# Top-k attention with a PReLU MLP: the MLP step ahead of the scores in a single block's tick, and k's copy at the end of PE's tick

## The chip, the cores and the metric

The kernel runs on 1 core of one Trainium2 chip. The metric is the device time of one execution in microseconds (us). Beside the times there is a profile: one execution recorded by the hardware profiler, with every instruction of the engines PE (TensorE), ACT (ScalarE), DVE (VectorE), POOL (GpSimd) and SP (SyncE, which here only issues DMAs).

## What is computed

The reference, cut to what matters. q, k and v are (8, 8, 576, 64) in float32: 8 batches of 8 heads of 576 rows.

```python
scores = scale * np.matmul(q, k.transpose(0, 1, 3, 2))
kth = np.partition(scores, -32, axis=-1)[..., -32:-31]
scores = np.where(scores >= kth, scores, -1e9)          # the 32 largest of each row of 576
attn = exp(scores - max(scores)); attn /= attn.sum() + 1e-9
x = matmul(attn, v)  ->  (8*576, 8*64)                  # 4608 tokens of 512
h = x @ w_in                                            # 512 -> 2048
out = (max(h, 0) + alpha * min(h, 0)) @ w_out           # 2048 -> 512
```

## The kernel before

**Tiling.** Two heads make a *pair*; there are 32 pairs, four to a batch. The 576 query rows of a pair's two heads are cut into nine *row blocks* of 128 rows: eight blocks of one head each (j = 0 to 7, heads alternating) and a ninth (j = 8) that holds the last 64 rows of both heads. A row block's scores are 128 x 576. There are 288 row blocks, and the schedule is a loop of ticks (line 861): in tick n each engine does its part for the row blocks that have come to it.

**Units.** Row blocks 0-1, 2-3, 4-5 and 6-7 go in units of two, and block 8 alone. The text calls block 8 a *single*, and its tick the single's tick. `scores(n0)` (line 312) does the score matmuls of a whole unit into PSUM tiles `ps` (two buffers). A unit of two needs both buffers, so the second of its tiles can only be written when ACT has copied the tile before it out.

**What each engine does with a row block.** PE: scores. ACT: `act_b` (L340, copies the scores to b with a per-row bias), `act_s` (L346, counts by sign how many are above a limit, the tile named h), `act_e` (L351, exp, once for a unit). POOL turns the count into a flip flag SG (L356). DVE then flips (y, L362), takes the 8 largest of five segments (L373), merges them (L387, L389), finds the limit, and makes the mask (mk, L436). POOL multiplies mask and exp (w, L446), and a DMA transposes w into wT (L459). PE multiplies wT by v (`av`, L497), DVE takes reciprocals of the sums (rz) and ACT scales the result into xb (L526). After the fourth pair of a batch, xb is transposed into xT by DMA and the MLP of that batch's tokens is queued.

**The MLP queue.** `back` is a list of MLP steps, at most one of which PE starts in a tick of the main part (lines 893 to 904). There are two kinds: a *ph step* (`ph_step`, L721: w_in times x into PSUM, after which ACT's relu, L727, makes gT) and a *pz step* (`pz_step`, L735 and L739: a third of the sum over w_id and w_out; after the third, ACT's L744 copies it to o_sb and SP writes it out). Each step goes into the one PSUM buffer "misc", so a new ph step, or the first third of a pz, waits until ACT has emptied it. ACT's part of a step (relu or copy) is put into `after` and is the first thing ACT does in the next tick. In the first 150 us the queue holds the preparation of the weights instead (`weight_steps`: L652 on ACT, L661 on PE).

**The preparation of a pair** (`prep_plan`, line 176) is laid out by hand over 14 ticks ahead of the pair's first row block: q's transposes on PE (`pe_q`, L198), their copy on ACT (`act_q`, L201) and k's transposes on PE (`pe_k`, L209) in the next tick, k's copy on ACT (`act_k`, L213) and the two remaining transposes (`pe_t`, L217 and L218) in the one after, then `act_t` (L221) and `pe_g` (L226), then `act_g` (L230, GK) and `pe_r` (L239, pr). All of them use one PSUM buffer "pa" in turn, up to pr, which has two banks of its own kind. `dve_p` (L245, L247: P from pr) follows on DVE a tick later. For nearly all pairs `pe_k` falls in a tick with j = 5, `act_k` in the next, j = 6, `act_g` and `pe_r` in the single's tick, and `dve_p` in the tick after it, j = 0. Pairs 11 and 20 (LEAD1, LEAD2) are four ticks earlier and use "misc".

**The order within a tick**, which is the order of each engine's instructions: PE does `scores(n + 1)`, if a unit starts at n + 1, then the MLP step, then `run(n, "pe")`: what the plan has put there (av, pe_q, pe_k, pe_r and so on). ACT does `after`, then `act_b` of a unit that starts at n; in a tick that starts a unit of two the plan's ACT work comes next and then `act_s`, in the unit's second tick `act_s`, the plan's ACT work and `act_e`, in a single's tick `act_b`, `act_s`, the plan's ACT work and `act_e`.

The ticks from 252 on (N0: the last four pairs) have another order of row blocks.

Of the kernel before, what the change touches and what calls it, by code (L numbers as in the profile page):

```python
# [31 lines left out]
def kernel(  # L32
# [20 lines left out]
    NT = NPAIR * TPP  # L53
# [7 lines left out]
    N0 = P0 * TPP  # L61
# [102 lines left out]
    n = 0  # L164
# [11 lines left out]
    def prep_plan(p):  # L176
# [117 lines left out]
        else:  # L294
            ts = [-14, -13, -12, -11, -10, -9, -7, -6, -5, -5, -4, -4, -3, -2, -8]
        dvx = "dve" if p < 2 else "dvx"
        steps = [dict(pe=[pe_q]), dict(act=[act_q], pe=[pe_k]), dict(act=[act_k], pe=[pe_t]),
                 dict(act=[act_t], pe=[pe_g]), dict(act=[act_g], pe=[pe_r]),
                 dict(dve=[dve_p]), dict(pe=[pe_s]), dict(act=[act_m]), dict(dve=[dve_2]),
                 {dvx: [dve_3]}, dict(dve=[dve_4]), {dvx: [dve_4b]}, dict(dve=[dve_5]),  # L300
# [473 lines left out]
    with tc.manual_schedule(engines={E.PE, E.Activation, E.DVE, E.Pool, E.SP}):  # L774
        cal = {}

        def put(tick, eng, f):
            cal.setdefault((tick, eng), []).append(f)

        def run(tick, eng):  # L780
            for f in cal.pop((tick, eng), ()):
                f()

        def plan(p):
            for dt, st in prep_plan(p):
                for eng, fs in st.items():
                    for f in fs:
                        put(BASE[p] + dt, eng, f)

        def feed(lim):  # L790
            while blocks and blocks[0][0] + blocks[0][1] <= lim:
                back.extend(mlp_steps(*blocks.pop(0)))

        def flush():
            while back:
                pe_f, act_f, _, takes = back.popleft()
                if takes and len(after) >= 2:
                    after.popleft()()
                pe_f()
                if act_f:  # L800
                    after.append(act_f)
            while after:
                after.popleft()()

        def tail_of(n, wn):
            wp, wj = ORDER[wn]
            b = wp // KPB
            if wp < P0:
                if wj == 3:
                    put(n + 3, "pe", lambda: av(wp, 0))  # L810
                    put(n + 4, "dve", lambda: av_rz(wp, 0))
                    put(n + 6, "act", lambda: av_out(wp, 0))
                    if wp % KPB == KPB - 1 and b >= 5:
                        put(n + 6, "end", lambda: x_turn(b, (0, 1)))
                        put(n + 8, "end", lambda: feed(b * S + 256))
                if wj == 8:
                    put(n + 4, "pe", lambda: av(wp, 1))
                    put(n + 5, "dve", lambda: av_rz(wp, 1))
                    put(n + 7, "act", lambda: av_out(wp, 1))
                    if wp % KPB == KPB - 1:  # L820
                        put(n + 7, "end", lambda: x_turn(b, range(2 if b >= 5 else 0, 5)))
                        put(n + 9, "end", lambda: feed((b + 1) * S))
            elif (wj == 8 or wj % 2) and wp % 2:
                i, g = wj // 2, (wp - P0) // 2
                dt = 2
                if i == 3 and g == 1:
                    put(n + dt, "pe", flush)
                put(n + dt, "pe", lambda: av_last(i, g))
                where = "end" if i == 3 and g == 0 else "dvx"
                put(n + dt + 1, where if where == "end" else "dve", lambda: rz_last(i, g))  # L830
                put(n + dt + 1, where, lambda: out_last(i, g))
                if i == 3:
                    if g == 1:
                        put(n + dt + 1, where, lambda: last_ph(0))
                    put(n + dt + 2 - g, where, lambda: turn_last(g))
                    if g == 1:
                        put(n + dt + 1, where, lambda: (last_ph(1), last_pz()))
                elif g == 1:
                    put(n + dt + 1, "dvx", lambda: x_turn(b, (i,)))
                    put(n + dt + 2, "end", lambda: back.extend(mlp_steps(*last.pop(i))))  # L840

        load(0, nc.scalar)
        load(1)
        load_alpha()
        plan(0)
        plan(1)
        early_sets()
        load_v(0)
        for t in range(-16, 0):
            for eng in ("act", "pool", "pe", "dve"):  # L850
                run(t, eng)
        scores(0)
        back = deque((a, c, 1.0, 0) for a, c in weight_steps())
        credit = 0.0
        after = deque()
        wdue, held = {}, []
        for wn in range(NT):
            wdue.setdefault(wn + LAG_W if wn < NW else 3 * (wn // 3) + 7, []).append(wn)
        n = 0
        end = max(NT + 24, 0)  # L860
        while n < end or back or after:
            if 8 <= n < 12:
                put(n, "end", lambda i=n - 8: load_v(1, [i]))
            for p in range(2, NPAIR):
                if n == max(0, BASE[p] - 18):
                    load(p)
                    plan(p)
                if n == max(0, BASE[p] - 13):
                    load_v(p)
            banks[0] = 2 if n >= NT else 1 if n >= N0 + 2 else 0  # L870
            if n + 1 < NT and unit_of[n + 1][2] == 0:
                scores(n + 1)
            while after:
                after.popleft()()
            if n < NT:
                n0, m, i = unit_of[n]
                if i == 0:
                    act_b(n0)
                    if m == 2:
                        run(n, "act")  # L880
                    act_s(n)
                    if m == 1:
                        run(n, "act")
                        act_e(n0)
                else:
                    act_s(n)
                    run(n, "act")
                    act_e(n0)
            run(n, "act")
            if n >= 3 and n % 3 == 0 and n - 3 < NT:  # L890
                sel_a((n - 3) // 3)
            nb = 1 if n < N0 + 2 else 2
            credit = min(credit, 0.0) + (2.4 if n >= NT else 1.9)
            first = True
            while back and credit > 0.0 and (first or nb == 2):
                pe_f, act_f, cost, takes = back[0]
                if takes and len(after) >= nb:
                    break
                back.popleft()
                pe_f()  # L900
                if act_f:
                    after.append(act_f)
                credit -= cost
                first = False
            run(n, "pe")
            if n >= NT:
                run(n, "dve")
                run(n, "dvx")
            due = wdue.get(n, ())
            for wn in due:  # L910
                if wn < NW:
                    mask(wn)
            for f in held:
                f()
            held = []
            for wn in due:
                weights(wn, wn >= NW)
                tail_of(n, wn)
            if 0 <= n - 1 < NT:
                side_of(n - 1)  # L920
            segs = seg_ops(n - LAG_S) if 0 <= n - LAG_S < NT else []
            mn = n - LAG_M
            merges = merge_ops(mn) if 0 <= mn < NT else []
            pick = bool(merges) and mn % 3 == 2
            if pick and n >= NT:
                sel_eq(mn // 3)
            lm = n - LAG_M - 3
            for i in range(max(len(segs), len(merges), 2)):
                if i < len(segs):
                    segs[i]()  # L930
                if i < len(merges):
                    merges[i]()
            run(n, "dve")
            if 0 <= lm < NT and lm % 3 == 0:
                limit(lm // 3)
            if pick and n < NT:
                sel_eq(mn // 3)
            if 0 <= n - 1 < NT:
                flip(n - 1)
            run(n, "dvx")  # L940
            if pick:
                sel_pr(mn // 3)
                held = [lambda m=mn // 3: sel_sum(m)]
                if mn % TPP == TPP - 1:
                    put(n + 2, "dve" if mn < NT - 1 else "end", lambda g=mn // TPP: check_group(g))
                    if mn == NT - 1:
                        put(n + 2, "end", checks)
                        put(n + 3, "end", final_flag)
                        put(n + 7, "end", read_flag)
            run(n, "end")  # L950
            n += 1
        assert not cal and not blocks and not last
# [138 lines left out]
```

## Time and profile before

| | us |
|---|---|
| time, median of 3 runs | 866.85 |
| the 3 runs | 864.89, 866.85, 867.13 |
| the profiled execution, its own time | 866.57 |
| its span, first to last instruction | 864.7 |
| PE busy with matmuls in the span | 711.5 (82%) |
| DVE busy | 817.5 (95%) |
| ACT busy | 783.7 (91%) |
| POOL busy | 443.6 (51%) |

The span is 1.87 us shorter than the execution's own time. The mean clock that the throttle granted to TensorE is 0.928 of full speed.

How to read the rows that follow. A row of the timeline gives the start in us from the span's start, the duration in us, the engine, the line of the kernel, the operation, out<-in, the shape, and how many equal instructions are merged in the row; in brackets the idle time of the engine just before it and what ended it. A row of the waits gives engine, line and tile, then what was waited for, then us in total, how often, and the longest. A matmul's end is modelled and overlaps the next one, and ACT's instructions overlap their neighbours by about 0.1 us. Float32 score matmuls appear as two instructions each, so a unit of two is x8.

### The profile page before, as it was taken

Reading aid. Unit: us, or ns where it says so; the run is one execution under the profiler, and the core shown is the slowest. Engines: PE = TensorE matmul, PEld = TensorE weight load, DVE = VectorE, ACT = ScalarE, POOL = GpSimd, SP = SyncE. Lnnn points to the kernel's source line nnn. Section 1 sums busy time; section 2 is a strip of 40 time slices with the busy share of each in tenths; the row PEclk is TensorE's granted clock in tenths of the full one; section 3 lists DMA queues with packets and bytes.
Section 4 is the critical chain, followed back from the end, with each engine's and each line's share of the span. In section 5 each row is a group of like instructions: output and inputs, shape, how many; then the busy total and the mean of one; then the engine's idle time right before and its main releaser. Section 6 shows DMA issues by size and latency. Waiting matters only on the chain. (4 is left out here: it accounts for less than half of the span.)

```text
span 864.7 us, 20335 instructions
## 1 busy us (share of the span) xinstructions
PE 711.5 (82%) x5696; PEld 424.3 (49%) x5771; DVE 817.5 (95%) x4901; ACT 783.7 (91%) x1865; POOL 443.6 (51%) x643
## 2 busy tenths in 40 slices
PE   5767688778968789877988789977897879899996
PEld 3434454434544445544454345644455455566674
DVE  5999999999999999999999999999999999998991
ACT  5989999989999999999999999999999799989861
POOL 5565555545545555554555545555555555554530
PEclk9666879889999999999997999999999899899998
DMA  7799965544775555564576456565456544435452
GB/s 144 141 162 183 168 116 102 120 97 87 137 142 119 91 116 127 108 123 90 116 162 113 96 97 130 110 126 104 100 116 126 114 100 90 94 77 96 100 91 52
DMA packets 343002, 99.06 MB, mean 115 GB/s; under 512 B 335056, under 2 KB 335328, under 8 KB 342880
## 3 DMA queue, kind: packets, MB, share of 16 engines
q1 hardware_dynamic: 338096, 94.99, 55.9%
q0 software_dynamic: 3584, 2.39, 2.2%
q8 instruction: 47, 0.77, 0.4%
q14 instruction: 75, 0.61, 0.2%
q10 hardware_dynamic: 1200, 0.30, 0.2%
HBM read 36.71 MB, written 9.44 MB: 53 GB/s over the span
## 5 line engine op out<-in xcount | busy, mean ns | idle before, releaser
L446 POOL TENSOR_TENSOR w<-mk,e 128x576 bf16<-128x576 bf16 x250 | 318.8, 1275 | 327.4 <-DVE mk L436 185.1
L373 DVE MAX8 C<-y 128x8 f32<-128x112 f32 (+1 forms) x1440 | 381.6, 265 | 0.1
L331 PE MATMUL ps<-qkT 64*128 64x288 f32 (+1 forms) x1280 | 254.1, 470 | 34.5 <-ACT b L340 33.8
L340 ACT ACTIVATE b<-ps,NT 128x576 f32<-128x576 f32 x288 | 202.1, 760 | 7.8 <-PE ps L331 7.8
L346 ACT ACTIVATE h<-b 128x576 bf16<-128x576 f32 x288 | 203.1, 705 | 1.6
L721 PE MATMUL ph<-xT,w_in_b 128*128 128x128 bf16 (+2 forms) x997 | 147.6, 289 | 41.6 <-ACT gT L727 38.4
L331 PEld LDWEIGHTS ps<-qkT 64*128 64x128 f32 (+1 forms) x1280 | 132.4, 192 | 95.4 <-ACT b L340 57.8
L351 ACT ACTIVATE e<-b 128x1152 bf16<-128x1152 f32 (+1 forms) x158 | 174.4, 1104 | 0.0
L362 DVE TENSOR_SCALAR y<-b,SG 128x576 int32<-128x576 int32 x288 | 149.4, 519 | 10.2 <-POOL SG L356 7.9
L387 DVE MAX8 L<-C 128x8 f32<-128x40 f32 x864 | 156.7, 181 | 0.1
L436 DVE TENSOR_SCALAR mk<-b,KP 128x576 bf16<-128x576 f32 x282 | 144.0, 511 | 0.0
L739 PE MATMUL pz<-w_out_b,gT 128*128 128x512 bf16 x542 | 132.6, 380 | 1.2 <-issue 0.5
L721 PEld LDWEIGHTS <-w_in_b 128*128 128x128 bf16 x1024 | 79.8, 99 | 104.2 <-issue 80.3
L727 ACT ACTIVATE gT<-ph 128x512 bf16<-128x512 f32 x140 | 85.8, 620 | 23.6 <-PE ph L721 23.4
L389 DVE MATCH_REPLACE8 C<-L,C 128x40 f32<-128x40 f32 x576 | 104.4, 181 | 0.0
L739 PEld LDWEIGHTS <-gT 128*128 128x128 bf16 x560 | 51.7, 98 | 68.9 <-issue 14.7
L497 PE MATMUL pu<-v_bf,wT 128*128 128x65 bf16 (+1 forms) x1600 | 68.8, 198 | 9.5 <-DMA wT<-w 9.1
L497 PEld LDWEIGHTS <-wT 128*128 128x128 bf16 (+1 forms) x1600 | 64.7, 103 | 18.8 <-DMA wT<-w 9.5
L356 POOL TENSOR_SCALAR SG<-S_all 128x1 int32<-128x1 f32 x288 | 64.8, 225 | 3.8 <-ACT h L346 3.5
L446 POOL TENSOR_TENSOR wm<-mk,e 128x576 bf16<-128x576 bf16 x32 | 40.8, 1276 | 46.3 <-DVE mk L436 43.7
L346 ACT ACTIVATION_READ_ACCUMULATOR h<-b 128x1 f32 x288 | 63.0, 219 | 0.0
L526 ACT ACTIVATE xb<-pu,rz 128x64 bf16<-128x64 f32 x224 | 54.4, 369 | 0.0
(116 smaller groups left out, 734.6 us busy)
## 6 DMA issues: line engine op xcount, KB each, us to landing
out_dram<-o_sb SPq DMA_DIRECT2D x34, 256.0 KB, 2.2
st_q<-in_q_dram SPq DMA_DIRECT2D x64, 128.0 KB, 2.8
kst<-in_k_dram SPq DMA_DIRECT2D x62, 128.0 KB, 2.9
st_v<-in_v_dram SPq DMA_DIRECT2D x60, 128.0 KB, 2.6
w_stage<-in_moe_w_out_dram SPq DMA_DIRECT2D x16, 256.0 KB, 3.2
w_in_b<-in_moe_w_in_dram POOLq DMA_DIRECT2D x8, 256.0 KB, 5.8
wT<-w SPq DMA_TRANSPOSE x128, 3.3
st_q<-in_q_dram SPq DMA_DIRECT2D x32, 32.0 KB, 2.6
```

The lines of the kernel that those rows point to most:

```text
L331: nc.tensor.matmul(o_, l_, r_, start=True, stop=True)
L340: nc.scalar.activation(t["b"].rearrange("p (a c) -> p a c", a=2), t["ps"], AF.Identity, bias=NT0[:, p * TPP + j:p * TPP + j + 1], scale=ON ...
L346: nc.scalar.activation(h, tiles[n]["b"], AF.Sign, accum_out=S_all[:, n:n + 1])
L351: nc.scalar.activation(e, tiles[n0]["bu"], AF.Exp, scale=scl)
L362: nc.vector.tensor_scalar(t["y"].bitcast(I32), t["b"].bitcast(I32), FLIP, SG[:, n:n + 1], ALU.bitwise_xor, ALU.bitwise_xor)
L373: return [lambda g=g: nc.vector.max(out=C[:, n % TPP, g, :], in_=y[:, g:S // 8:NSEG, :]) for g in range(NSEG)]
L387: ops.append(lambda r=r, src=src: nc.vector.max(out=L[:, 8 * r:8 * r + 8], in_=src))
L436: nc.vector.tensor_scalar(t["mk"], t["b"], row_limit(n), None, ALU.is_ge)
L446: nc.gpsimd.tensor_tensor(dst, t["mk"], t["e"], ALU.mult)
L497: nc.tensor.matmul(o_, wT[:, 4 * side + c, cs], d["v"][:, 5 * side + c, :], start=(c == 0), stop=(c == 4))
L721: nc.tensor.matmul(hold[f][:, i, :], w_in_b[:, kk, (f + i) * 128:(f + i + 1) * 128], xT[:, kk, c0:c0 + tb], start=(kk == 0), stop=(kk == N ...
L739: nc.tensor.matmul(pz[0:m], hold["gT"][:, f, r0:r0 + m], w_out_b[:, f, :], start=False, stop=(f == NFT - 1))
```

## The change

Two things move; no instruction is added or taken away.

1. In the tick of a single (j = 8) before tick 252, where the next unit's scores are due, `scores(n + 1)` is now emitted behind the MLP step of that tick instead of ahead of it. The plan's PE work (`pe_r`) still comes last. That is 28 ticks, one for each pair up to the 28th. In all other ticks the scores stay first.
2. `act_k` moves from the plan's ACT work of the tick after `pe_k` to a new slot "actz" at the end of ACT's work in the tick of `pe_k` itself. On ACT's queue it now stands ahead of the next tick's `after` and `act_b`, and behind `act_e`. This holds for pairs 1 to 31; pair 0 has a plan of its own.

```diff
-        steps = [dict(pe=[pe_q]), dict(act=[act_q], pe=[pe_k]), dict(act=[act_k], pe=[pe_t]),
+        steps = [dict(pe=[pe_q]), dict(act=[act_q], pe=[pe_k], actz=[act_k]), dict(pe=[pe_t]),
...
-            if n + 1 < NT and unit_of[n + 1][2] == 0:
+            nxt = n + 1 < NT and unit_of[n + 1][2] == 0
+            late = nxt and n < N0 and unit_of[n][1] == 1
+            if nxt and not late:
                 scores(n + 1)
             while after:
                 after.popleft()()
...
                 credit -= cost
                 first = False
+            if late:
+                scores(n + 1)
             run(n, "pe")
+            run(n, "actz")
```

## The prediction, made before the changed kernel was run

> **What bounds the kernel now.** First the page: which engine is full, and what the chain that ended last is made of.
>
> ```profile
> PE 711.5 (82%) x5696; PEld 424.3 (49%) x5771; DVE 817.5 (95%) x4901; ACT 783.7 (91%) x1865; POOL 443.6 (51%) x643
> ...
> PE 12%; ACT 4%; DVE 1%; issue 0%; DVEq 0%
> ```
>
> DVE is nearly full, yet the chain that ended last holds 16% of the span on PE and ACT and 1% on DVE: the last stretch hangs on when PE and ACT get there. So two things run side by side, DVE, and a loop of PE and ACT that wait for one another. Second, the waits from 130 us (first MLP steps) to 730 us (the last tick that the change touches), ACT's and then DVE's:
>
> ```profile
> ACT gT L727 <- PE ph L721: 18.1, 18, 2.7
> ACT o_sb L744 <- PE pz L739: 9.2, 6, 1.6
> ```
>
> ```profile
> DVE P L247 <- PE pr L239: 9.3, 11, 1.9
> ```
>
> ACT waits only for PE here, never for DVE, so ACT and PE go at a pace of their own; DVE loses 9.3 us in 11 waits for pr, which PE makes in a single's tick, and under 1.5 us in smaller rows. What PE and ACT gain reaches the end, as long as DVE follows; DVE can follow by about those 9.3 to 10.5 us.
>
> Third, the timeline of one single's tick whose MLP step is a ph step; ACT, PE, DVE:
>
> ```profile
> 391.20 0.68 ACT L727 ACTIVATE gT<-ph 128x512 bf16<-128x512 f32 x1
> 391.67 0.83 ACT L340 ACTIVATE b<-ps,NT 128x576 f32<-128x576 f32 x1
> ...
> 393.38 0.67 ACT L351 ACTIVATE e<-b 128x576 bf16<-128x576 f32 x1
> 394.80 0.60 ACT L727 ACTIVATE gT<-ph 128x512 bf16<-128x512 f32 x1 [0.75 <-PE ph L721]
> 395.29 1.36 ACT L340 ACTIVATE b<-ps,NT 128x576 f32<-128x576 f32 x2
> ```
>
> ```profile
> 392.56 1.24 PE L331 MATMUL ps<-qkT 64*128 64x288 f32 x6 [1.73 <-ACT b L340]
> 393.72 1.04 PE L721 MATMUL ph<-xT,w_in_b 128*128 128x512 bf16 x4
> 394.69 0.44 PE L239 MATMUL pr<-qkT,GK 64*64 64x512 bf16 x4
> ```
>
> ```profile
> 395.15 0.82 DVE L247 TENSOR_TENSOR P<-pr,qkT 128x512 bf16<-128x512 f32 x2 [0.86 <-PE pr L239]
> ```
>
> PE idles 1.73 us until the single's b has freed the second score buffer, does the scores, and only then ph, whose buffer had been free since the relu ended at 391.88. ACT runs dry for ph and DVE for pr.
>
> **The change part by part. Part 1, ph singles.** After it, ph starts at the relu's end, about 391.93, and ends near 392.95, beside b; the scores follow (b ended at 392.50) to about 394.2, then pr to 394.6 instead of 395.13. ACT's gT starts at e's end, its 0.75 us of waiting gone; b comes 0.5 us behind gT's start, at about 394.5, and the scores are there by 0.3 us. That margin is the cover; without it the wait moves to b. Of the 18 gT waits, four stand at the head of a single's tick, on the ph of the tick before, and stay; the first and the last of them:
>
> ```profile
> 159.66 0.60 ACT L727 ACTIVATE gT<-ph 128x512 bf16<-128x512 f32 x1 [0.95 <-PE ph L721]
> ...
> 569.95 0.60 ACT L727 ACTIVATE gT<-ph 128x512 bf16<-128x512 f32 x1 [0.59 <-PE ph L721]
> ```
>
> With the two between, 2.7 us. The other 14 hold 15.4. Three of these are long because PE ran at half clock, here the one at 676 us (rows of PE, of ACT, and the stretch with its granted clock, 0.50, as the third number from the end), then ACT's rows of the other two:
>
> ```profile
> 672.05 2.29 PE L331 MATMUL ps<-qkT 64*128 64x288 f32 x6 [1.71 <-ACT b L340]
> 674.27 1.89 PE L721 MATMUL ph<-xT,w_in_b 128*128 128x256 bf16 x8
> ```
>
> ```profile
> 676.20 0.60 ACT L727 ACTIVATE gT<-ph 128x512 bf16<-128x512 f32 x1 [2.65 <-PE ph L721]
> ```
>
> ```profile
> 672.00:677.90 5.90, 5.56 (x20) 2.90 (x22) 5.53 (x34) 3.22 (x7) 2.92 (x4) 0.50 0.59 122
> ```
>
> ```profile
> 191.46 0.60 ACT L727 ACTIVATE gT<-ph 128x512 bf16<-128x512 f32 x1 [2.65 <-PE ph L721]
> ...
> 497.73 0.60 ACT L727 ACTIVATE gT<-ph 128x512 bf16<-128x512 f32 x1 [2.21 <-PE ph L721]
> ```
>
> Eleven at full clock: 15.4 - 2.65 - 2.21 - 2.65 = **7.9 us**, all gained by ACT. In the three slow ones, kept slow, the scores end last: 1.9 for ph from 0.6 ahead of b's end, 2.3 for the scores, so ACT's b can start 3.6 after the single's b, against 4.7: 1.1 us in one, 1.85 in the half-slow one at 497, and 0.5 in the one at 676, where PE itself is behind afterwards. Together **3.4 us**; with the clock at full they would give 7.5, with none of it kept 0.
>
> **Part 1, pz singles.** Six singles (one in each batch from 213 us, the last at 725) have a pz step. ACT, then PE:
>
> ```profile
> 416.67 0.62 ACT L744 COPY o_sb<-pz 128x512 f32<-128x512 f32 x1
> 417.13 0.80 ACT L340 ACTIVATE b<-ps,NT 128x576 f32<-128x576 f32 x1
> ...
> 419.38 1.36 ACT L340 ACTIVATE b<-ps,NT 128x576 f32<-128x576 f32 x2
> ...
> 425.43 0.58 ACT L744 COPY o_sb<-pz 128x512 f32<-128x512 f32 x1 [1.51 <-PE pz L739]
> ```
>
> ```profile
> 417.98 1.24 PE L331 MATMUL ps<-qkT 64*128 64x288 f32 x6 [0.81 <-ACT b L340]
> 419.15 1.04 PE L735 MATMUL pz<-w_id_b,xT 128*128 128x512 bf16 x4
> 420.02 0.81 PE L739 MATMUL pz<-w_out_b,gT 128*128 128x512 bf16 x3
> 420.76 0.44 PE L239 MATMUL pr<-qkT,GK 64*64 64x512 bf16 x4
> ```
>
> Here ACT didn't wait: b started at 419.38 with its scores ready. Now pz runs from 417.35 to 418.96, the scores to 420.2, pr to 420.5. So **b waits 0.85 us that it didn't wait before**, and behind it on ACT stand h and e of that unit. But pr and all that follows on PE come 0.7 us earlier, and 6 us later ACT stands 1.51 us waiting for PE's pz (the o_sb waits, 9.2 us in 6): the lost 0.85 is eaten there, and PE's 0.7 comes through. 6 x 0.7 = **4.2 us**; if the o_sb wait didn't cover it, it would be 6 x 0.85 = 5.1 lost instead. At 726 us PE becomes the chain that ends last, so the sixth counts in full too.
>
> Singles without an MLP step stay as they are. `scores` issues no DMA; the DMAs and POOL work of the weight steps that it is moved behind keep their order on SP and POOL.
>
> **Part 2, k's copy.** It costs 0.5 us on ACT wherever it stands, so its place matters only through waiting. At the end of j = 5 it waits for k's transposes, and behind it stand the relu or o_sb copy, both b and h, and PE's next MLP step behind the relu. The gain, pt no longer waiting on PE, I put at nothing: the scores and the MLP step after it wait for ACT anyway; that cover gone it would be at most 0.9 a pair. In most pairs k's transposes end as ACT gets there:
>
> ```profile
> 410.33 1.24 ACT L351 ACTIVATE e<-b 128x1152 bf16<-128x1152 f32 x1
> ```
>
> ```profile
> 410.92 0.60 PE L209 MATMUL pk<-ident_f,kst 128*128 128x128 f32 x4
> ```
>
> ACT could start at 411.47, the transposes end at 411.52: 0.1 us or none. In five ticks (one in each batch, just after the pz steps) PE is late:
>
> ```profile
> 434.78 1.20 ACT L351 ACTIVATE e<-b 128x1152 bf16<-128x1152 f32 x1
> ...
> 437.09 0.61 ACT L213 COPY qkT<-pk 128x512 f32<-128x512 f32 x1
> ```
>
> ```profile
> 436.21 0.60 PE L209 MATMUL pk<-ident_f,kst 128*128 128x128 f32 x4
> ```
>
> ACT would start at 435.85 and gets k at 436.85: 1.0 us lost, where it now does both b first and finds k ready. 5 x 1.0 = 5, and about 1.2 for all others together: **6.2 us lost**, from 0, if a wait further on takes it up, to twice that.
>
> In the weight stage PE is later still, held by the wT transposes on the DMA queue (PE, ACT):
>
> ```profile
> 75.92 0.73 PE L497 MATMUL pu<-v_bf,wT 128*128 128x65 bf16 x10 [3.23 <-DMA wT<-w]
> ...
> 79.63 1.06 PE L209 MATMUL pk<-ident_f,kst 128*128 128x128 f32 x4
> ```
>
> ```profile
> 78.20 0.76 ACT L652 ACTIVATE xT<-w_stage,alpha_sb 128x512 bf16<-128x512 f32 x1
> 78.90 1.37 ACT L340 ACTIVATE b<-ps,NT 128x576 f32<-128x576 f32 x2
> 80.73 0.58 ACT L213 COPY qkT<-pk 128x512 f32<-128x512 f32 x1 [0.45 <-PE pk L209]
> ```
>
> What ACT did from 78.20 to 80.15 now comes behind the copy at 80.73: **1.9 us lost**, and ACT is full from there on. Two such ticks before it lose as much, but PE's DMA wait at 75.92 takes that back. Ends: 0 and 4.
>
> **Sum**: 7.9 + 3.4 + 4.2 - 6.2 - 1.9 = 7.4 us. Without the early 1.9, PE and ACT gain 9.3, which is what DVE waits. From the profiled execution's own 866.57 (0.28 below the median): **859.2 us**.
>
> **The rivals.**
> *The waits only change their names* (no change). ACT's b waits for the scores where gT waited for ph. For it: the six pz singles, and a margin of only 0.3 us in the others. If the o_sb wait doesn't take up the 0.85, the sum loses 5.1 + 4.2: 859.2 + 9.3 = 868.5; with some given back, 867.
>
> *ACT stops for k* (slower). Place: the head of ACT's queue at the end of j = 5. Price: 1.0 us in five ticks now, 2.4 where PE runs at half clock (80.69 against 78.25 in the rows above). It decides from 7.4 / 31 = 0.24 us more lateness in the mean of all 31 copies; five more half-clock ticks of that kind bring 859.2 + 12 = 871. Against it: k's transposes mostly follow q's copy by 0.7 us while e takes 1.2.
>
> *The clock stays up* (faster). PE's idle before the late scores goes, and the three slow singles with it: 4.1 more, of which DVE, which can follow only by 10.5 - 1.9, lets through about 1; with no early loss as well, 856. The Trainium skill ("TensorE: Matmul & The Clock Gate", Part 1: The HAM clock gate) says that the clock halves after an idle window of about 3.4 us. By that rule these ticks would never be slow, before or after, and this rival holds. The trace disagrees: granted 0.50 at 672 with a longest wait of 1.71. So slow ticks may as well move elsewhere, and I keep them.
>
> **How the numbers follow.** Forecast 0.62 (857 to 863), the clock 0.08, names changed 0.15, ACT stops for k 0.15. Within 0.3% (2.6 us) is about what a measurement of this kernel can't tell from no change. Faster 0.70, same 0.15, slower 0.15. The range reaches from the rival below, 855.5, to the no-change rival's 867.5, and leaves out most of the slower one.
>
> **What would show it.** Right: at j = 0 no gT wait on ACT (14 now), b waiting 0.8 for the scores in the six pz singles, o_sb waits shorter, pr waits of DVE nearly gone, a new ACT wait of k's copy for pk of 5 to 8 us in the run. Wrong: DVE still waiting for pr, b's waits for ps above 6 us, ACT's wait for pk above 12, or more half-clock stretches after 130 us.

## The result, and the profile after

The changed kernel takes 862.23 us in the median of 7 runs (858.77 to 863.01), the kernel before 865.34 in as many runs beside it (864.89 to 867.13). The ratio on record is 0.9939, with a 95% interval of 0.9924 to 0.9955: faster by 0.6%, which is outside the 0.3% that can't be told from no change. The ratios given here and below are not quotients of medians: 0.6% would be 5.3 us, and the two medians are 3.1 us apart (quotient 0.9964), so the size of the gain is known to about 2 us only. The forecast was 859.2 with a range of 855.5 to 867.5. The profiled execution took 862.69, with a span of 860.8.

ACT's and then DVE's waits of the changed kernel between 130 and 730 us:

```profile
ACT b L340 <- PE ps L331: 10.0, 12, 1.3
ACT qkT L213 <- PE pk L209: 9.3, 9, 1.8
ACT gT L727 <- PE ph L721: 1.0, 2, 0.7
ACT o_sb L744 <- PE pz L739: 0.6, 1, 0.6
```

```profile
DVE P L247 <- PE pr L239: 1.6, 6, 0.6
```

ACT's wait for ph fell from 18.1 us to 1.0, its wait for pz from 9.2 to 0.6, DVE's wait for pr from 9.3 to 1.6. In their place stand two others: b for the scores, 10.0 us (1.2 before), and k's copy for k's transposes, 9.3 us (none before). Both are larger than the prediction had them: it took more than 6 us for the first as a sign of being wrong, and expected 5 to 8 for the second.

The same ph single as in the prediction, now (ACT, PE, DVE):

```profile
393.61 0.69 ACT L727 ACTIVATE gT<-ph 128x512 bf16<-128x512 f32 x1
394.08 0.83 ACT L340 ACTIVATE b<-ps,NT 128x576 f32<-128x576 f32 x1
...
395.79 0.67 ACT L351 ACTIVATE e<-b 128x576 bf16<-128x576 f32 x1
396.36 0.59 ACT L727 ACTIVATE gT<-ph 128x512 bf16<-128x512 f32 x1
396.84 1.37 ACT L340 ACTIVATE b<-ps,NT 128x576 f32<-128x576 f32 x2
```

```profile
394.34 1.02 PE L721 MATMUL ph<-xT,w_in_b 128*128 128x512 bf16 x4 [1.84 <-ACT gT L727]
395.30 1.24 PE L331 MATMUL ps<-qkT 64*128 64x288 f32 x8
396.47 0.44 PE L239 MATMUL pr<-qkT,GK 64*64 64x512 bf16 x4
```

```profile
396.92 0.69 DVE L247 TENSOR_TENSOR P<-pr,qkT 128x512 bf16<-128x512 f32 x1 [0.18 <-PE pr L239]
```

The unit's b (396.84) starts 2.76 us after the single's b, against 3.62 before, without a wait in front of it. PE's work runs through, from ph over the scores to pr.

A pz single, now (ACT, PE):

```profile
418.38 0.63 ACT L744 COPY o_sb<-pz 128x512 f32<-128x512 f32 x1
418.85 0.81 ACT L340 ACTIVATE b<-ps,NT 128x576 f32<-128x576 f32 x1
...
421.94 1.37 ACT L340 ACTIVATE b<-ps,NT 128x576 f32<-128x576 f32 x2 [0.74 <-PE ps L331]
...
426.51 0.59 ACT L744 COPY o_sb<-pz 128x512 f32<-128x512 f32 x1
```

```profile
419.06 1.02 PE L735 MATMUL pz<-w_id_b,xT 128*128 128x512 bf16 x4 [1.39 <-ACT o_sb L744]
419.93 0.81 PE L739 MATMUL pz<-w_out_b,gT 128*128 128x512 bf16 x3
420.67 1.24 PE L331 MATMUL ps<-qkT 64*128 64x288 f32 x8
421.84 0.44 PE L239 MATMUL pr<-qkT,GK 64*64 64x512 bf16 x4
```

b waits 0.74 us that it didn't wait before, and the 1.51 us in front of the second o_sb are gone: from the single's b to that o_sb it is 7.66 us, against 8.30.

These two ticks went as forecast. Most of the 3 us that are missing was lost before 120 us. DVE's first P of pair 5, after and before (the kernel counts pairs from 0; the first expectation below calls it the fifth):

```profile
119.33 0.69 DVE L247 TENSOR_TENSOR P<-pr,qkT 128x512 bf16<-128x512 f32 x1 [0.51 <-PE pr L239]
```

```profile
114.69 0.69 DVE L247 TENSOR_TENSOR P<-pr,qkT 128x512 bf16<-128x512 f32 x1 [0.39 <-PE pr L239]
```

The stage up to there takes 4.64 us longer, where the forecast had 1.9; from there to the end the span is 8.5 us shorter, where it had 9.3.

### The profile page after: what moved, and what is told of

Read it like the earlier page. It is cut to its first block, busy times and chain, and to the rows that moved or that the text cites. A ratio compares the mean times of both kernels' runs of the same rounds, so it can differ in the third digit from the quotient of the medians.

```text
span 860.8 us, 20304 instructions
## 1 busy us (share of the span) xinstructions
PE 710.3 (83%) x5696; PEld 427.5 (50%) x5771; DVE 817.3 (95%) x4901; ACT 786.1 (91%) x1865; POOL 444.2 (52%) x643
## 5 line engine op out<-in xcount | busy, mean ns | idle before, releaser
L331 PE MATMUL ps<-qkT 64*128 64x288 f32 (+1 forms) x1280 | 246.7, 478 | 19.7 <-ACT b L340 19.3
```

The lines of the kernel that those rows point to most:

```text
L331: nc.tensor.matmul(o_, l_, r_, start=True, stop=True)
```

## The experiments

All times are medians beside runs of the kernel before on the same chip: 866.87 in the first group of four, 866.91 in the second, 866.45 in the last two. The changed kernel's 862.23 was measured beside 865.34, in a group of its own, so a difference between it and a time below is uncertain by about 1.6 us.

**The scores alone.** k's copy goes back to its old place.

```diff
-        steps = [dict(pe=[pe_q]), dict(act=[act_q], pe=[pe_k], actz=[act_k]), dict(pe=[pe_t]),
+        steps = [dict(pe=[pe_q]), dict(act=[act_q], pe=[pe_k]), dict(act=[act_k], pe=[pe_t]),
```

> Only the scores move (k's copy stands in the tick after, as before). Theory (part 1 earns all, part 2 only costs): the early delay, in which DVE's first P of the fifth pair starts at 119.3 us after the change against 114.7 before, goes; ACT's waits of k's copy for pk (16.6 us in the changed kernel) fall to under 1; PE and ACT gain some 15 us, of which DVE can follow by the 9 to 10.5 us of its waits: 855 to 858 us. Rival (part 1 only turns ACT's wait for ph into a wait for scores, and the gain is from PE no longer waiting for k's copy): 864 to 867 us.

Measured: 854.23 us, ratio 0.9857 (0.9842 to 0.9872). This is 1.4% below the kernel before, and below the changed kernel too. The stretch from pair 5's P to the tick where the change ends, first of this kernel, then of the kernel before (the columns: length, busy time of PE, PEld, DVE, ACT and POOL with their instruction counts, granted clock, DMA share, GB/s):

```profile
115.00:718.00 603.00, 507.77 (x4053) 297.76 (x4113) 601.14 (x3640) 585.10 (x1429) 322.94 (x455) 0.95 0.59 116
```

```profile
115.00:729.00 614.00, 515.80 (x4036) 297.40 (x4098) 602.42 (x3642) 583.18 (x1424) 323.15 (x456) 0.96 0.57 114
```

DVE is busy for 601.1 of 603.0 us: it has become the bound. ACT still waits 15.6 us from 130 to 730 us in the four largest rows of its waits, and with DVE idle for less than 2 us that can hardly reach the end. The theory holds; the time is a little under its 855 to 858.

**k's copy alone.** The scores stand first again.

```diff
-            late = nxt and n < N0 and unit_of[n][1] == 1
+            late = False
```

> Only k's copy moves (the scores stand first in a single's tick, as before). Theory: the early delay of 4.6 us stays, and from 130 us on PE and ACT lose about 6 us more in waits of k's copy for pk, with nothing earned: DVE's waits for pr grow by as much, 873 to 878 us. Rival (k's copy earns by freeing the buffer of PE's transposes, whose wait for it was 27.1 us): 859 to 864 us.

Measured: 884.25 us, ratio 1.0219 (1.0201 to 1.0238). The direction is that of the theory, the size is not: 17 us lost where 6 to 11 were expected. (The five runs reach from 878.70 to 887.46, and the profile is of the fastest.) The last two runs take this up.

**k's copy in the late pairs, and in the early pairs.** Both with the late scores. The new place holds for pairs 7 to 31 in one and for pairs 1 to 6 in the other.

```diff
+        kq, kt = (dict(actz=[act_k]), dict()) if p > 6 else (dict(), dict(act=[act_k]))   # or: p <= 6
-        steps = [dict(pe=[pe_q]), dict(act=[act_q], pe=[pe_k], actz=[act_k]), dict(pe=[pe_t]),
+        steps = [dict(pe=[pe_q]), dict(act=[act_q], pe=[pe_k], **kq), dict(pe=[pe_t], **kt),
```

> As the changed kernel, but k's copy stands as before in pairs 1 to 6 (the weight stage) and is moved in pairs 7 to 31 alone. Theory: the early 4.6 us come back and reach the end, as nothing behind them takes them up: 857 to 858.5 us, with DVE's waits before 130 us back to those of the kernel before. Rival (the late stage sets the end, and the early delay was taken up there): 861 to 863 us.

> As the changed kernel, but k's copy is moved in pairs 1 to 6 alone and stands as before in pairs 7 to 31. Theory: the early 4.6 us stay lost, while ACT's waits for pk after 130 us (9.3 us) go: 860 to 862 us, later than the kernel with the scores alone by 3.5 to 5 us. Rival (the early delay doesn't reach the end): within 1 us of the kernel with the scores alone.

Measured: 858.75 us for the late pairs (ratio 0.9904, 0.9889 to 0.9920), 857.98 for the early ones (0.9899, 0.9884 to 0.9914). Against the scores alone, in the same group, the late pairs cost 4.5 us and the early pairs 3.75; the two add up to the 8 us between the scores alone (854.2) and the whole change (862.2), as far as two groups can be compared. The early delay reaches the end, and by twice the forecast. The early kernel came out some 2 us below what was expected of it, the late one just above. Both costs count from a kernel whose bound is DVE, so they are what reaches the end and not all that ACT and PE lose.

**The pz singles.** Once the whole change without them, once they alone on the kernel before.

```diff
             late = nxt and n < N0 and unit_of[n][1] == 1
+            late = late and not (back and back[0][2] == 1.5)          # the change, without the pz singles
+            late = late and bool(back) and back[0][2] == 1.5          # they alone, k's copy as before
```

> As the changed kernel, but in the six singles whose MLP step is a pz step the scores stand first again. Theory (the late pz scores earn 0.7 us each on PE, ACT's wait of 0.73 behind them is taken up by the o_sb wait): ACT's six waits of b for the scores go, its waits of o_sb for pz come back at 1.5 us each, and the time rises by 2 to 4.5 us over the changed kernel's 862.2, to 864 to 867. Rival (the wait for the scores is a plain loss): 856 to 860.

> The kernel before, with the scores moved in the six pz singles alone and nothing else. Theory: PE and ACT gain 6 x 0.7 = 4.2 us, DVE's waits for pr fall by as much: 861.5 to 864 against 866.9. Rival (b's new wait of 0.85 is lost): 867 to 872.

Measured: 864.62 us (0.9970, 0.9953 to 0.9988) without them, and 861.22 (0.9936, 0.9914 to 0.9959) with them alone: six moves of eight score instructions behind a pz step give 5.7 us, although each adds a wait on ACT. The 2.4 us by which the first lies above the changed kernel compare two groups and say little alone; in its profile ACT's waits of o_sb for pz are back, at 13.0 us in six. The second is a comparison within one group, and a little better than the 861.5 that it was expected to reach. ACT's waits from 130 to 730 us in the kernel with the six alone:

```profile
ACT gT L727 <- PE ph L721: 19.6, 17, 2.4
ACT b L340 <- PE ps L331: 4.4, 6, 0.7
ACT o_sb L744 <- PE pz L739: 1.2, 1, 1.2
```

Six new waits of b hold 4.4 us, and the o_sb waits fall by 8.0 from the 9.2 of before. The rival, by which the wait for the scores is a plain loss, is wrong in both runs.

**k's transposes ahead, so that the copy needn't wait.** In pairs 7 to 31 q comes a tick earlier and k's transposes stand ahead of the MLP step; the copy stays at the end of that tick.

```diff
-        steps = [dict(pe=[pe_q]), dict(act=[act_q], pe=[pe_k], actz=[act_k]), dict(pe=[pe_t]),
+        steps = [dict(pe=[pe_q]), dict(act=[act_q], pe=[pe_k]), dict(act=[act_k], pe=[pe_t]),
...
-        return list(zip(ts, steps))
+        plan_ = list(zip(ts, steps))
+        if p > 6:
+            plan_[0:3] = [(-15, dict(pe=[pe_q])), (-14, dict(act=[act_q])),
+                          (-13, dict(pe0=[pe_k], actz=[act_k])), (-12, dict(pe=[pe_t]))]
+        return plan_
...
+            run(n, "pe0")
             nb = 1 if n < N0 + 2 else 2
```

> As the changed kernel, but in pairs 7 to 31 q's transposes and copy come a tick earlier and k's transposes stand ahead of the MLP step, so that k's copy at the end of the tick finds them done; in pairs 1 to 6 k's copy stands as before. Theory (k's copy costs only by its wait for pk): ACT's waits of k's copy for pk after 130 us fall from 7.8 us (moved in the late pairs alone) to under 1, and the time from 858.75 to 854 to 855.5, that of the scores moved alone. Rival (the place itself costs, since b stands behind the copy): 858 to 860.

Measured: 854.13 us, ratio 0.9855 (0.9832 to 0.9879). ACT's wait of the copy for pk from 130 us on, in the kernel with the late pairs moved and in this one:

```profile
ACT qkT L213 <- PE pk L209: 7.8, 10, 1.1
```

```profile
ACT qkT L213 <- PE pk L209: 1.4, 2, 1.2
```

With most of the wait gone its cost is gone, all 4.5 us, at the same place on ACT's queue. What reached the end was that ACT gets there before k does. (The wait didn't quite fall under 1 us.) It isn't faster than the scores alone, since DVE is the bound in both; a small cost of the place itself would not show here, and q's and k's steps on PE were moved too.

**The scores late in every tick** that starts a unit, on top of the scores alone.

```diff
-            late = nxt and n < N0 and unit_of[n][1] == 1
+            late = nxt and n < N0
```

> The scores alone, moved behind the MLP step in every tick before 252 that starts a unit and not in the singles' alone. Theory (the move earns only where the scores wait for ACT's b of the same tick while the MLP step could start; in the other ticks the score buffers are long free, and the MLP step is what waits, for ACT's relu): ACT's waits of b for ps rise from 6 us to 15 or more after 130 us, above all behind pz steps, and the time rises from 854.2 to 856 to 862. Rival (the MLP step first is better wherever it stands, since it feeds ACT): 850 to 854.

Measured: 866.46 us, ratio 0.9998 (0.9984 to 1.0011): 12 us above the scores alone, more than expected. ACT's largest wait from 130 us on, with the scores alone it is gT for ph at 7.5 us, and here:

```profile
ACT b L340 <- PE ps L331: 24.5, 34, 1.2
```

Moved everywhere, the reordering gives back all that it earned in the 28 singles.

**k's copy alone, in the late and in the early pairs.** What is open is why the copy costs 17 us by itself and 8 beside the late scores.

```diff
         kq, kt = (dict(actz=[act_k]), dict()) if p > 6 else (dict(), dict(act=[act_k]))   # or: p <= 6
...
+            late = False
```

> The kernel before, with k's copy moved in pairs 7 to 31 alone; the scores stand first in a single's tick. On top of the late scores these pairs cost 4.3 to 4.5 us (859 against 854.2, 862.2 against 858). Theory (with the scores first, PE idles for the single's b, more half-clock stretches fall on the singles, and DVE has no slack, so the same move costs more): 874 to 881 us against 866.9, with DVE waits for pr above 1.3 us each where the granted clock is 0.5. Rival (the costs add up): 870 to 873.

> The kernel before, with k's copy moved in pairs 1 to 6 alone; the scores stand first in a single's tick. Theory (the early delay adds up whatever comes later): 870 to 872 us against 866.9, by the 3.5 to 3.8 us that it costs on top of the late scores. Rival (it is part of what makes the copy cost 17 us by itself): 874 or more; rival (it is taken up later): 866 to 868.

Measured: 882.36 us for the late pairs (ratio 1.0192, 1.0166 to 1.0217), 871.89 for the early ones (1.0070, 1.0045 to 1.0094). The early delay reaches the end here too, with a little more than 5 us. The late pairs cost 15.9 us where they cost 4.5 beside the late scores, and the time lies above the 874 to 881 that were expected. The two costs, 21.3 us, are more than the 17.4 of both moves at once, so they don't simply add up. DVE's wait for pr in that kernel between 130 and 730 us, and four half-clock stretches of it, each behind the 3.4 us that lead up to it:

```profile
DVE P L247 <- PE pr L239: 21.4, 16, 2.1
```

```profile
209.60:213.00 3.40, 2.06 (x14) 1.09 (x10) 3.40 (x20) 3.37 (x8) 1.47 (x2) 1.00 0.26 82
213.00:216.40 3.40, 3.40 (x10) 1.07 (x11) 1.61 (x14) 3.40 (x9) 1.47 (x2) 0.50 1.23 119
260.80:264.20 3.40, 1.82 (x21) 1.12 (x19) 3.39 (x23) 3.40 (x12) 2.31 (x3) 1.00 0.90 171
264.20:271.00 6.80, 6.03 (x18) 2.30 (x18) 4.97 (x31) 4.32 (x13) 2.10 (x4) 0.50 0.71 150
472.40:475.80 3.40, 1.21 (x11) 0.68 (x7) 3.39 (x22) 3.40 (x10) 2.13 (x4) 1.00 0.81 151
475.80:482.60 6.80, 6.64 (x20) 2.41 (x20) 4.74 (x26) 4.32 (x14) 1.55 (x3) 0.50 0.79 159
680.60:684.00 3.40, 1.83 (x15) 1.19 (x13) 3.39 (x23) 3.40 (x10) 2.26 (x3) 1.00 0.90 162
684.00:690.80 6.80, 6.30 (x22) 3.18 (x24) 5.43 (x31) 4.12 (x11) 2.19 (x5) 0.50 0.67 141
```

In these stretches DVE is busy 1.61 of 3.40, 4.97, 4.74 and 5.43 of 6.80 us, and ACT idles in the three longer ones. Eight of DVE's 16 waits for pr are above 1.3 us, and all eight start in a half-clock stretch or end just behind one. From 130 to 730 us the mean granted clock is 0.93 there and 0.96 in the kernel before. So the waits are as the theory has them, but they don't account for the whole: DVE waits 12.1 us more for pr than in the kernel before, of 15.9 us lost. Why more of these stretches fall on the singles there wasn't tried and stays open; and one profile of each kernel can't say how often they do.

## Why the prediction was right, and which terms were mis-sized

*What bounds the kernel.* Right: PE and ACT form a loop of their own, whose gains reach the end as long as DVE follows. With the scores alone, the loop gets so far ahead that DVE is busy all along, and 11.0 us are gained between 115 us and the end of the changed ticks, close to the bound of 9 to 10.5 that was read from DVE's waits. The whole change comes near that bound as well; the changed kernel over the same work:

```profile
119.30:725.60 606.30, 503.76 (x4041) 295.09 (x4101) 602.57 (x3643) 584.11 (x1423) 323.52 (x456) 0.95 0.57 115
```

DVE idles for 3.7 us here, against 11.6 of 614.0 before. So the late stage came out near its 9.3 us, which was also what DVE could follow by, and the time doesn't check the late terms one by one. The 15.5 us of part 1 show in no run: alone it gives 12.6, with DVE in front of the rest.

*Ph singles, 7.9 and 3.4 us.* The mechanism is shown, the sizes were not measured by themselves: gT's wait is gone, and pr and b come earlier by about the working's amounts (the unit's b stands 0.86 us closer to the single's b, where the working had 0.8). That slow clock would stay was right too, only that it sits elsewhere: of b's 12 waits for the scores six are the pz singles' at 0.7, and the other six hold 5.6 us, five of them starting in a half-clock stretch. These five are why the sum of b's waits passed the 6 us that the prediction named.

*Pz singles, 4.2 us.* Right, and the point on which the no-change rival hung: b waits 0.74, the o_sb wait takes it up. Alone they give 5.7 us, with 4.2 inside the interval (3.6 to 7.5).

*k's copy in the late pairs, 6.2 us lost.* Right in kind; 4.5 and 4.2 us reach the end in the two comparisons with late scores. The five late copies wait 0.86 us each, one of them here (ACT):

```profile
437.92 0.59 ACT L213 COPY qkT<-pk 128x512 f32<-128x512 f32 x1 [0.86 <-PE pk L209]
```

They make 4.3 of the 9.3 us. The other four waits hold 5.0, where the prediction put 1.2 for all others; two of them start in half-clock stretches. So the waits were put too low, and yet less than 6.2 us reached the end. Both comparisons start from a kernel in which DVE is the bound; how much ACT and PE lose behind that isn't separated.

*k's copy in the weight stage, 1.9 us lost.* This is the step that failed, and most of the 3 us by which the forecast missed, counted by stage: 3.75 us in the runs, 4.64 in the profile. The prediction counted one late copy of three, "but PE's DMA wait at 75.92 takes that back". It doesn't. The changed kernel's DVE at the first, ACT at the second, PE at that DMA wait:

```profile
33.19 0.17 DVE L272 TENSOR_TENSOR sq<-M,sq 128x9 f32<-128x9 f32 x1 [2.20 <-ACT M L268]
```

```profile
57.09 0.59 ACT L213 COPY qkT<-pk 128x512 f32<-128x512 f32 x1 [4.81 <-PE pk L209]
```

```profile
79.19 0.49 PE L497 MATMUL pu<-v_bf,wT 128*128 128x65 bf16 x10 [2.00 <-DMA wT<-w]
```

The first copy already makes DVE wait 2.2 us. DVE's first P of pairs 2, 3 and 4, each behind one more such copy, starts 1.9, 3.1 and 4.5 us later than before. In these profiles the first two copies thus cost 3.1 us and the third 1.4. The wait for wT is shorter by 1.2 (2.00 for 3.23) but ends 3.3 us later: wT comes from w, and at that time DVE's masks and POOL's w are already 3.1 us late. This wait on a DMA took up nothing, since what is moved was itself delayed.

The clock may have a part in it: up to 114 us the mean granted clock is 0.64 in the changed kernel and 0.75 before, and 0.68 to 0.70 in the other four kernels with the early move against 0.70 to 0.76 in the other six without it. Whether that is a cause of the delay or follows from it isn't separated.

Counted by parts instead of stages, the two terms for k's copy make 8.1 us in the forecast and about 8 in the runs. That this sum fits is luck: the early term was too small, and of the late one only a part came through.

*Part 2 earns nothing.* Right, and shown best by the kernel without it: part 1 by itself is 8 us faster than the whole change.

*The slower rival* (ACT stops for k) did not decide here. By itself the copy's move costs 17 us, but not as this rival has it: ACT's waits of the copy for k between 130 and 730 us are 9.2 us there and 9.3 in the changed kernel. What is larger is DVE's wait for pr, 17.4 us against 1.6.

## What to carry to other kernels

When an engine's queue holds a step that waits for another engine in this tick and one that is free to run, put the free one first, and only there: the same order in the ticks whose scores waited for nobody cost 12 us. A new wait was free where a longer wait stood behind it on the same engine (0.74 us ahead of 1.5); follow the engine to its next wait. Before a copy is moved up, compare the end of what it reads with the time at which its engine gets there, and above all in the stage that has its delays from elsewhere.

## What the runs showed of the hardware

The granted clock of TensorE fell to 0.50 without an idle window. In the four cases above PE was busy 1.21 to 2.06 of the 3.4 us ahead of the drop, and its longest wait there was 1.3 to 1.9 us. The Trainium skill ("TensorE: Matmul & The Clock Gate", Part 1: The HAM clock gate) has it fall after an idle window of about 3.4 us; the drops here come in lengths of 3.4 and 6.8 us, which fits such a window, but the windows ahead of them were not idle. The measurement decides: with PE busy for 36 to 61% of such a stretch, a drop has to be reckoned with. It doesn't always come: in the changed kernel PE is busy 1.56 us from 391.2 to 394.6, and the clock stays at 1.00 in the 3.4 us behind. What share of busy time is enough to hold it was not measured.
